# Blocks with one tile of tokens: the first expert product in another orientation, and two paddings

## The chip, the core and the metric

The kernel runs on one core of a Trainium2 chip. The metric is device time in microseconds (us) of that core, from runs of the whole program; one more execution was taken with the hardware profiler. The core has a matrix engine (TensorE; PE in the profile, PEld for its loads of the stationary operand), VectorE (DVE), ScalarE (ACT), GpSimd (POOL) and SyncE (SP, which issues most DMAs). A matmul holds a 128x128 stationary operand in the array and streams the moving operand past it; the result goes to PSUM.

## What is computed

Three stages follow each other on 4608 tokens of width 512:

```python
# chunked attention on q, k, v of (8, 8, 576, 64), chunks of 64; out -> x (4608, 512)
h = max(x @ w1, x @ w2, x @ w3); x = h @ w_out            # moe_: 512 -> 768 -> 512
e_idx = argmax(x @ w_gate, axis=1)                        # moe2_: 8 experts
gate_w = softmax(x @ w_gate)[row, e_idx]; eom = sigmoid(x @ w_output_gate)
for e in range(8):
    mask = e_idx == e
    h = maximum(x[mask] @ w1[e], 0)                       # 512 -> 1024
    out[mask] = gate_w[mask, None] * eom[mask, e, None] * (h @ w2[e])   # 1024 -> 512
```

## The kernel before

All products are in 32-bit floats, each as three matmuls: an operand is kept as a high part (rounded for the array) and a low part (the rest), and `mm3` (L101 to L104) multiplies high by high (L102), high by low (L103) and low by high (L104).

Up to some 710 us the kernel does attention and the first mixture, with instructions that a small planner in the program has put in order. In that stage tokens are taken in 9 blocks of 512; `moe_f` (L613) streams the tokens of block j, 512 columns, past 128x128 tiles of w1, w2, w3. There are 18 such tiles of 4 steps, so 18 x 4 x 3 = 216 matmuls for each of the 9 blocks. The tokens lie in `xt[j % 2]`, high and low part: `xth0`, `xtl0` for even j, `xth1`, `xtl1` for odd j. `moe_y` makes the product with w_out, 256 and 272 columns wide, 432 x 3 = 1296 matmuls, with tiles `ht` as the stationary operand.

Then come the experts. Tokens are sorted by expert and taken in blocks of at most 256 of one expert; block b holds one or two tiles of 128 tokens. `step(b)` does a block:

- `l1_mm`: for each of the 8 tiles of 128 hidden units, the weight tile is stationary and 256 token columns stream past it (4 steps x 3 matmuls): 96 matmuls into four PSUM banks (mm0, mm1, mm2, psg). `l1_hi` (ACT, relu) and `l1_lo` (DVE) put the result, hidden units on the partitions, into `hT` as high and low part. All 256 columns are computed whether the second tile has tokens or not.
- `x_T(b + 1)`: eight PE transposes turn the next block's tokens into `xs`, by way of the PSUM tile a2.
- `l2(b, t)`: for tile t, 24 matmuls of 512 columns with `hT` stationary and w2 moving; the result goes to tr0 (t = 0) or tr1. The second tile is inside `tc.If(full[b] > 0)`, a branch of PE alone: a block with one tile skips it.
- `y_act` (ACT) scales the result, `y_out` (POOL) scatters it to the output by an indirect DMA. `gather_ahead` (POOL) fetches the tokens of block b + 2.
- `switch(b, ns)`: where block b is the last of its expert (`lv > 0`), the weights of the next expert are converted from the raw tiles to high and low parts, `conv_hi` on ACT and `conv_lo` on DVE, four instructions each for every one of the four raw tiles; then SP issues `load_x` for the raw tiles of the expert after that, 1 MB each. Raw tiles 0 and 1 (w1) are converted inside the block, 2 and 3 (w2) at its end, behind `y_act(b, 1)`.

Each engine works through its own instructions in order and waits on semaphores. Tiles of the pool `p1` lie behind each other in SBUF in the order in which the program makes them; `xg01` (the gathered tokens) takes the place of `xth1` and is a little larger than it, 2 x 2 x 516 floats against 2048. The built program before puts the first weight tile `wpc0` at byte 20288 of a partition, `xth0` at 153472, `xtl0` at 161664, `xth1` at 169856 and `xtl1` at 178112.

Of the kernel before, what the change touches and what calls it, by code (L numbers as in the profile page):

```python
# [10 lines left out]
F32 = mybir.dt.float32  # L11
# [4 lines left out]
ACTF = mybir.ActivationFunctionType  # L16
# [5 lines left out]
def tile_chunk_attention_moe_moe(  # L22
# [16 lines left out]
    PE, ACT, DVE, POOL, SP = nc.tensor, nc.scalar, nc.vector, nc.gpsimd, nc.sync  # L39
# [55 lines left out]
    def f(ap):  # L95
        return ap.bitcast(F32)

    def sub(eng, o, a, b):
        eng.tensor_tensor(out=o, in0=a, in1=b, op=ALU.subtract)  # L99

    def mm3(o, ah, al, bh, bl, first, last):  # L101
        PE.matmul(o, ah, bh, start=first, stop=False)  # L102
        PE.matmul(o, ah, bl, start=False, stop=False)  # L103
        PE.matmul(o, al, bh, start=False, stop=last)  # L104
# [63 lines left out]
    def buf(shape, dtype, name):  # L168
        return p1.tile(shape, dtype, name=name, tag=name)
# [10 lines left out]
    pTF = [part(3, i, 1).rearrange("p (a c i) -> p a c i", a=HP, c=2) for i in range(2)]  # L180
    NV = len(v_buf)
    mxs, sms = ([buf([P, H], F32, f"{n}{i}") for i in range(NE2)] for n in ("mx", "sm"))
    XN = KD * TB * P
    xtn = lambda hl, i: f"xt{'hl'[hl]}{i}"
    xtile = lambda hl, i: p1.tile([P, KD, TB * P], F32R, name=xtn(hl, i), tag=xtn(hl, i))
# [593 lines left out]
    def xkeys(i, *hls):  # L779
# [6 lines left out]
        [("pTF", i) for i in range(2)] + [("cy", i) for i in range(2)],  # L786
    ]
    raw = [Late(ar, f"R{n}", [P, 4, DM], F32, f"raw{n}", akeys[n]) for n in range(4)]
    xg01 = Late(p1, xtn(0, 1 - lastx), [P, 2, 2, XW], F32, "xg01",
                xkeys(1 - lastx, 0) + [("xg", i, t) for i in range(2) for t in range(2)])  # L790
    xs0 = Late(p1, xtn(1, 1 - lastx), [P, 2, KD, BP], F32R, "xs0", xkeys(1 - lastx, 1) + [("xs0", i) for i in range(4)])
    xg2 = Late(wp, f"P{NFT // 4}", [P, 2, XW], F32, "xg2", [("w", n, hl) for n in range(16, NFT) for hl in range(2)])
# [23 lines left out]
    ]  # L816
    xsk = [[("xs0", i) for i in range(4)], [("wo", i) for i in range(8, 12)]]
    hTk = [("wo", i) for i in range(8)]
    xg = lambda b: xg2.t if b % NX == 2 else xg01.t[:, b % NX]
    yo = lambda b, t: yol[2 * (b % 2) + t].t  # L820
    bk = [("mm", 0), ("mm", 1), ("mm", 2), ("mm", 0)]
    ps_x = ps_a2.rearrange("p (a b) -> p a b", a=KD)
# [3 lines left out]
    def load_x(n, e, cond):  # L826
        src = (
            ew1_v[:, bass.ds(e, 1), :, n * DM:(n + 1) * DM] if n < 2
            else ew2_v[:, bass.ds(e, 1), (n - 2) * 4:(n - 1) * 4, :]
        )  # L830
        kw = {} if cond is None else {"cond": cond > 0}
        SP.dma_start(out=raw[n].t, in_=src.rearrange("p o k f -> p (o k) f"), **kw)

    def sval(engines, row, b, hi):
        return nc.values_load(  # L835
            sched_i()[0:1, row * NBLK + b:row * NBLK + b + 1], engines=engines, min_val=0, max_val=hi
        )
# [4 lines left out]
    def conv_lo(n, kk):  # L842
        sub(DVE, wx[n][:, 1, kk], raw[n].t[:, kk], f(wx[n][:, 0, kk]))
# [28 lines left out]
    def l1_mm(b, c, i):  # L872
        x, ps = xs[b % 2](), l1_ps(c)
        w, ff = wx[c // 2], ((2 * c + i) % 4) * P
        for kk in range(KD):
            mm3(
                ps[:, i], w[:, 0, kk, ff:ff + P], w[:, 1, kk, ff:ff + P], x[:, 0, kk], x[:, 1, kk],
                kk == 0, kk == KD - 1,
            )

    def l1_hi(c):
        ACT.activation(out=hT()[:, 0, 2 * c:2 * c + 2], in_=l1_ps(c), func=ACTF.Relu)  # L882

    def l1_lo(c):
        fs = slice(2 * c, 2 * c + 2)
        DVE.scalar_tensor_tensor(  # L886
            out=hT()[:, 1, fs], in0=l1_ps(c), scalar=0.0, in1=f(hT()[:, 0, fs]), op0=ALU.max, op1=ALU.subtract
        )

    def l2_mm(t, ff):  # L890
        sl = slice(t * P, (t + 1) * P)
# [6 lines left out]
    def y_act(b, t):  # L898
        ACT.activation(out=yo(b, t), in_=ps_y[t], func=ACTF.Copy, scale=xg(b)[:, t, DM:DM + 1])  # L899

    def y_out(b, t):
        POOL.indirect_dma_start(  # L902
            out=out, out_offset=bass.IndirectOffsetOnAxis(ap=ic[b % 4]()[:, t, 1:2].bitcast(U32), axis=0),
            in_=yo(b, t), in_offset=None, bounds_check=NT - 1, oob_is_err=False,
        )
# [223 lines left out]
    def x_T(b):  # L1129
        if b < NBLK:  # L1130
            xT_mm(b)
            for i in range(2):
                xT_hi(b, i)
                xT_lo(b, i)

    def switch(b, ns):


        lv, cl, en = meta[b]
        with tc.If(lv > 0):  # L1140
            for n in ns:
                for kk in range(4):
                    conv_hi(n, kk)
                    conv_lo(n, kk)
        for n in ns:
            load_x(n, en, cl)

    def scalars(b):
        meta[b] = (
# [9 lines left out]
    def l2(b, t):  # L1159
        for ff in range(2 * KD):  # L1160
            l2_mm(t, ff)
        if t == 0:
            y(b, t)

    def y(b, t):
        y_act(b, t)
        y_out(b, t)

    def step(b):
        scalars(b)  # L1170
        gather_ahead(b + 2)
        if b >= NB0:
            POOL.drain()  # L1173
        for c in range(4):
            for i in range(2):
                l1_mm(b, c, i)
            l1_hi(c)
            l1_lo(c)
            if c == 2:
                switch(b, (0,))  # L1180
        x_T(b + 1)
        switch(b, (1,))
        if b + 1 < NBLK:
            full[b + 1] = sval([ET.PE], 7, b + 1, 1)
        l2(b, 0)
        with tc.If(full[b] > 0):
            l2(b, 1)
        y(b, 1)
        switch(b, (2, 3))

    e1 = nc.values_load(next_i()[0:1, 0:1], engines=[ET.SP], min_val=0, max_val=E - 1)
    h0 = nc.values_load(next_i()[0:1, NBLK:NBLK + 1], engines=[ET.SP], min_val=0, max_val=1)
    for n in range(4):
        load_x(n, e1, h0)
    scalars(0)
    full = {1: sval([ET.PE], 7, 1, 1)}
    switch(0, (0,))
    l2(0, 0)
    x_T(1)
    switch(0, (1,))  # L1200
    l2(0, 1)
# [57 lines left out]
```

## Time and profile before

| | |
|---|---|
| median of 3 runs | 1191.08 us (1190.87 to 1193.05) |
| profiled execution | 1190.56 us |
| its span, first to last instruction | 1188.8 us |
| PE busy | 1172.4 us (99%) |
| PEld busy | 1035.3 us (87%) |
| DVE busy | 432.5 us (36%) |
| ACT busy | 416.3 us (35%) |
| POOL busy | 194.4 us (16%) |

The span is 1.8 us shorter than the profiled execution's own time: what lies around the instructions. A matmul's duration in the profile is longer than the distance to the next one, since matmuls are pipelined; so what a matmul costs is read from start to start. The granted TensorE clock was 0.998 over the span, where 1.0 is 2.4 GHz and 0.5 is 1.2 GHz.

### The profile page before, as it was taken

The numbers are of one execution on the slowest core, as the hardware profiler recorded it, in microseconds if no ns is written. First come the engines' busy times: TensorE is split into PE (matmuls) and PEld (weight loads), VectorE is DVE, ScalarE is ACT, GpSimd is POOL, SyncE is SP. The second block draws the span as 40 slices with busy tenths as digits, with TensorE's granted clock in tenths as the row PEclk, the third lists the DMA queues.
The fourth block names the chain that finished last, engine by engine and source line by source line (L and its number), as shares of the span: only waits on it lengthen the run. The fifth ranks groups of instructions, "written<-read, shape, count | busy, mean of one in ns | idle before, by whom it ended". The sixth has DMA issues, their size and how long they took to land. (4 is left out here: it accounts for less than half of the span.)

```text
span 1188.8 us, 23369 instructions
## 1 busy us (share of the span) xinstructions
PE 1172.4 (99%) x9219; PEld 1035.3 (87%) x9219; DVE 432.5 (36%) x1095; ACT 416.3 (35%) x1192; POOL 194.4 (16%) x243
## 2 busy tenths in 40 slices
PE   7999999999999999999999999999999999999997
PEld 6779889898898988989889898989999998998997
DVE  6995523232232322322223352121165221521172
ACT  5576323332333333333322321221266221521263
POOL 1000120211102111021110112212212211211212
PEclk9999999999999999999999999999999999999999
DMA  8753212112121121211230015211256411421151
GB/s 276 236 150 103 82 38 89 45 42 76 38 85 36 48 70 51 73 45 34 75 107 36 1 46 183 76 37 45 64 176 233 146 36 46 161 70 45 57 172 39
DMA packets 84317, 103.05 MB, mean 87 GB/s; under 512 B 40287, under 2 KB 49503, under 8 KB 84192
## 3 DMA queue, kind: packets, MB, share of 16 engines
q1 hardware_dynamic: 77152, 79.82, 21.0%
q0 software_dynamic: 7040, 21.60, 5.6%
q8 instruction: 75, 1.23, 0.4%
q14 instruction: 50, 0.41, 0.1%
HBM read 149.55 MB, written 20.52 MB: 143 GB/s over the span
## 5 line engine op out<-in xcount | busy, mean ns | idle before, releaser
L102 PE MATMUL mm<-xth,wpc 128*128 128x512 f32 x576 | 231.4, 402 | 0.0
L103 PE MATMUL mm<-xtl,wpc 128*128 128x512 f32 x576 | 226.3, 393 | 0.2 <-DVE xtl L99 0.2
L104 PE MATMUL mm<-xth,wpc 128*128 128x512 f32 x576 | 226.3, 393 | 0.0
L628 DVE TENSOR_TENSOR hs<-mm,hs 128x512 f32<-128x512 f32 x108 | 74.5, 690 | 226.9 <-PE mm L104 226.9
L886 DVE SCALAR_TENSOR_TENSOR wo<-mm,wo 128x512 fp32r<-128x512 f32 x64 | 43.6, 690 | 240.1 <-ACT wo L882 206.6
L104 PEld LDWEIGHTS mm<-xth,wpc 128*128 128x128 f32 x576 | 108.4, 188 | 24.5
L102 PEld LDWEIGHTS mm<-xth,wpc 128*128 128x128 f32 x576 | 108.2, 188 | 23.5
L103 PEld LDWEIGHTS mm<-xtl,wpc 128*128 128x128 f32 x576 | 108.4, 188 | 22.3 <-DVE xtl L99 0.5
L102 PE MATMUL mm<-wo,ht 128*128 128x256 f32 (+1 forms) x432 | 125.6, 291 | 0.0
L104 PE MATMUL mm<-wo,ht 128*128 128x256 f32 (+1 forms) x432 | 122.7, 284 | 0.0
L103 PE MATMUL mm<-wo,ht 128*128 128x256 f32 (+1 forms) x432 | 122.6, 284 | 0.0
L102 PE MATMUL tr<-wpc,wo 128*128 128x512 f32 x304 | 120.2, 396 | 0.0
L104 PE MATMUL tr<-wpc,wo 128*128 128x512 f32 x304 | 118.5, 390 | 0.0
L103 PE MATMUL tr<-wpc,wo 128*128 128x512 f32 x304 | 118.4, 389 | 0.0
L902 POOL DMA_INDIRECT out_dram<-yo,S x42 | 43.9, 1044 | 352.7 <-ACT yo L899 268.6
L99 POOL TENSOR_TENSOR ht<-hs,ht 128x512 fp32r<-128x512 f32 x48 | 61.9, 1290 | 192.3 <-ACT ht L630 192.3
L465 ACT ACTIVATE rg<-a,mx 128x64 f32<-128x64 f32 x264 | 79.3, 326 | 34.5 <-DVE mx L459 34.4
L99 DVE TENSOR_TENSOR wpc<-raw,wpc 128x512 fp32r<-128x512 f32 x112 | 70.3, 685 | 39.8 <-ACT wpc L840 39.8
L102 PEld LDWEIGHTS mm<-wo,ht 128*128 128x128 f32 x432 | 81.3, 188 | 1.3 <-issue 0.4
L882 ACT ACTIVATE wo<-mm 128x512 fp32r<-128x512 f32 x64 | 38.2, 598 | 124.8 <-PE mm L104 119.3
L103 PEld LDWEIGHTS mm<-wo,ht 128*128 128x128 f32 x432 | 81.5, 189 | 0.4
L104 PEld LDWEIGHTS mm<-wo,ht 128*128 128x128 f32 x432 | 81.3, 188 | 0.0
(243 smaller groups left out, 2252.7 us busy)
## 6 DMA issues: line engine op xcount, KB each, us to landing
raw<-in_moe_w_dram SPq DMA_DIRECT2D x92, 1024.0 KB
x_scratch<-U SPq DMA_DIRECT2D x36, 258.0 KB
rg<-in_q_dram SPq DMA_DIRECT2D x36, 256.0 KB
rg<-in_k_dram SPq DMA_DIRECT2D x36, 256.0 KB
wst<-in_moe_w_dram SPq DMA_DIRECT2D x18, 512.0 KB
rg<-in_v_dram SPq DMA_DIRECT2D x128, 64.0 KB
U<-in_moe_w_out_dram SPq DMA_DIRECT2D x6, 512.0 KB
rg<-in_v_dram SPq DMA_DIRECT2D x4, 256.0 KB
```

Source lines behind the costliest of these rows:

```text
L99: eng.tensor_tensor(out=o, in0=a, in1=b, op=ALU.subtract)
L102: PE.matmul(o, ah, bh, start=first, stop=False)
L103: PE.matmul(o, ah, bl, start=False, stop=False)
L104: PE.matmul(o, al, bh, start=False, stop=last)
L465: ACT.activation(out=ex[:, b, hp], in_=bank[b][:, hp], func=ACTF.Exp, scale=scale, bias=mx[:, HP * b + hp:HP * b + hp + 1], accum_out=sm[: ...
L628: add("DVE", t_dve(N), up, [pk, hk], [hk], lambda: DVE.tensor_tensor(out=h, in0=ps, in1=h, op=ALU.max))
L882: ACT.activation(out=hT()[:, 0, 2 * c:2 * c + 2], in_=l1_ps(c), func=ACTF.Relu)
L886: DVE.scalar_tensor_tensor(out=hT()[:, 1, fs], in0=l1_ps(c), scalar=0.0, in1=f(hT()[:, 0, fs]), op0=ALU.max, op1=ALU.subtract)
L902: POOL.indirect_dma_start(out=out, out_offset=bass.IndirectOffsetOnAxis(ap=ic[b % 4]()[:, t, 1:2].bitcast(U32), axis=0), in_=yo(b, t), in_ ...
```

## The change

In a block with one tile of tokens the first product is computed the other way round. The tokens are the stationary operand and w1 is the moving one, 512 columns wide (`h_mm`), so the result has tokens on the partitions; ACT takes the relu to SBUF (`h_relu`, in a part of the tile `U`), eight PE transposes bring it into two PSUM banks (`h_T`), and `hT_hi` (ACT) and `hT_lo` (DVE) write `hT` as before. Blocks with two tiles keep their instructions. For this the branch on `full[b]` now stands at the head of the block, on PE, ACT and DVE, with an Else; conversions are inside it, loads (`fetch`) behind it. Two paddings move tiles of `p1`: a tile of 48 floats behind the small attention tiles, and rows of 544 instead of 516 floats in `xg01`, which makes that slot 8704 bytes instead of 8256. The built program now has `xth0` at 153664, `xtl0` at 161856, `xth1` at 170048 and `xtl1` at 178752; `wpc0` stays at 20288.

```diff
--- before.py
+++ after.py
@@ -180,6 +180,8 @@
     pTF = [part(3, i, 1).rearrange("p (a c i) -> p a c i", a=HP, c=2) for i in range(2)]
     NV = len(v_buf)
     mxs, sms = ([buf([P, H], F32, f"{n}{i}") for i in range(NE2)] for n in ("mx", "sm"))
+
+    buf([P, 48], F32, "pad")
     XN = KD * TB * P
     xtn = lambda hl, i: f"xt{'hl'[hl]}{i}"
     xtile = lambda hl, i: p1.tile([P, KD, TB * P], F32R, name=xtn(hl, i), tag=xtn(hl, i))
@@ -786,7 +788,7 @@
         [("pTF", i) for i in range(2)] + [("cy", i) for i in range(2)],
     ]
     raw = [Late(ar, f"R{n}", [P, 4, DM], F32, f"raw{n}", akeys[n]) for n in range(4)]
-    xg01 = Late(p1, xtn(0, 1 - lastx), [P, 2, 2, XW], F32, "xg01",
+    xg01 = Late(p1, xtn(0, 1 - lastx), [P, 2, 2, 544], F32, "xg01",
                 xkeys(1 - lastx, 0) + [("xg", i, t) for i in range(2) for t in range(2)])
     xs0 = Late(p1, xtn(1, 1 - lastx), [P, 2, KD, BP], F32R, "xs0", xkeys(1 - lastx, 1) + [("xs0", i) for i in range(4)])
     xg2 = Late(wp, f"P{NFT // 4}", [P, 2, XW], F32, "xg2", [("w", n, hl) for n in range(16, NFT) for hl in range(2)])
@@ -816,7 +818,7 @@
     ]
     xsk = [[("xs0", i) for i in range(4)], [("wo", i) for i in range(8, 12)]]
     hTk = [("wo", i) for i in range(8)]
-    xg = lambda b: xg2.t if b % NX == 2 else xg01.t[:, b % NX]
+    xg = lambda b: xg2.t if b % NX == 2 else xg01.t[:, b % NX, :, 0:XW]
     yo = lambda b, t: yol[2 * (b % 2) + t].t
     bk = [("mm", 0), ("mm", 1), ("mm", 2), ("mm", 0)]
     ps_x = ps_a2.rearrange("p (a b) -> p a b", a=KD)
@@ -886,6 +888,32 @@
         DVE.scalar_tensor_tensor(
             out=hT()[:, 1, fs], in0=l1_ps(c), scalar=0.0, in1=f(hT()[:, 0, fs]), op0=ALU.max, op1=ALU.subtract
         )
+
+
+    hh = U[:, 0:2 * DM].bitcast(F32).rearrange("p (g n) -> p g n", g=2)
+
+    def h_mm(b, g):
+        x, w = xs[b % 2](), wx[g]
+        for kk in range(KD):
+            mm3(
+                ps_mm[g], x[:, 0, kk, 0:P], x[:, 1, kk, 0:P], w[:, 0, kk], w[:, 1, kk], kk == 0, kk == KD - 1
+            )
+
+    def h_relu(g):
+        ACT.activation(out=hh[:, g], in_=ps_mm[g], func=ACTF.Relu)
+
+    def h_T(g):
+        for i in range(4):
+            PE.transpose(ps_mm[2 + g][:, i * P:(i + 1) * P], hh[:, g, i * P:(i + 1) * P], ident)
+
+    def h_out(hl, g):
+        return hT()[:, hl, 4 * g:4 * g + 4, 0:P]
+
+    def hT_hi(g):
+        ACT.copy(h_out(0, g), ps_mm[2 + g].rearrange("p (a i) -> p a i", a=4))
+
+    def hT_lo(g):
+        sub(DVE, h_out(1, g), ps_mm[2 + g].rearrange("p (a i) -> p a i", a=4), f(h_out(0, g)))
 
     def l2_mm(t, ff):
         sl = slice(t * P, (t + 1) * P)
@@ -1133,17 +1161,22 @@
                 xT_hi(b, i)
                 xT_lo(b, i)
 
-    def switch(b, ns):
-
-
-        lv, cl, en = meta[b]
-        with tc.If(lv > 0):
+    def convs(b, *ns):
+
+        with tc.If(meta[b][0] > 0):
             for n in ns:
                 for kk in range(4):
                     conv_hi(n, kk)
                     conv_lo(n, kk)
+
+    def fetch(b, ns):
+
         for n in ns:
-            load_x(n, en, cl)
+            load_x(n, meta[b][2], meta[b][1])
+
+    def switch(b, ns):
+        convs(b, *ns)
+        fetch(b, ns)
 
     def scalars(b):
         meta[b] = (
@@ -1159,8 +1192,6 @@
     def l2(b, t):
         for ff in range(2 * KD):
             l2_mm(t, ff)
-        if t == 0:
-            y(b, t)
 
     def y(b, t):
         y_act(b, t)
@@ -1171,31 +1202,52 @@
         gather_ahead(b + 2)
         if b >= NB0:
             POOL.drain()
-        for c in range(4):
-            for i in range(2):
-                l1_mm(b, c, i)
-            l1_hi(c)
-            l1_lo(c)
-            if c == 2:
-                switch(b, (0,))
-        x_T(b + 1)
-        switch(b, (1,))
+        with tc.If(full[b] > 0) as both:
+            for c in range(4):
+                for i in range(2):
+                    l1_mm(b, c, i)
+                l1_hi(c)
+                l1_lo(c)
+                if c == 2:
+                    convs(b, 0)
+            x_T(b + 1)
+            convs(b, 1)
+            l2(b, 0)
+            y_act(b, 0)
+            l2(b, 1)
+        with both.Else():
+
+            for g in range(2):
+                h_mm(b, g)
+                if g:
+                    convs(b, 0)
+                h_relu(g)
+            for g in range(2):
+                h_T(g)
+                hT_hi(g)
+                hT_lo(g)
+            x_T(b + 1)
+            convs(b, 1)
+            l2(b, 0)
+            y_act(b, 0)
+        fetch(b, (0, 1))
         if b + 1 < NBLK:
-            full[b + 1] = sval([ET.PE], 7, b + 1, 1)
-        l2(b, 0)
-        with tc.If(full[b] > 0):
-            l2(b, 1)
+            full[b + 1] = sval(FULL, 7, b + 1, 1)
+        y_out(b, 0)
         y(b, 1)
-        switch(b, (2, 3))
+        convs(b, 2, 3)
+        fetch(b, (2, 3))
 
     e1 = nc.values_load(next_i()[0:1, 0:1], engines=[ET.SP], min_val=0, max_val=E - 1)
     h0 = nc.values_load(next_i()[0:1, NBLK:NBLK + 1], engines=[ET.SP], min_val=0, max_val=1)
     for n in range(4):
         load_x(n, e1, h0)
     scalars(0)
-    full = {1: sval([ET.PE], 7, 1, 1)}
+    FULL = [ET.PE, ET.Activation, ET.DVE]
+    full = {1: sval(FULL, 7, 1, 1)}
     switch(0, (0,))
     l2(0, 0)
+    y(0, 0)
     x_T(1)
     switch(0, (1,))
     l2(0, 1)
```

ACT, in the program before, one block in the expert stage from its first relu to the conversions at its end (L840 is `conv_hi`, L882 `l1_hi`, L862 the next block's tokens, L899 `y_act`; mm_156 to mm_158 and psg are the four banks):

```order
L882 ACTIVATE wo<-mm_156 128x512
L882 ACTIVATE wo<-mm_157 128x512
L882 ACTIVATE wo<-mm_158 128x512
L1140 COMPARE_AND_BRANCH
L840 CAST wpc_142<-raw_5878 128x512 x4
L1140 UNCONDITIONAL_BRANCH x2
L882 ACTIVATE wo<-psg 128x512
L862 CAST wo<-a_155 128x512 x2
L1140 COMPARE_AND_BRANCH
L840 CAST wpc_143<-raw_6006 128x512 x4
```

The four casts of raw tile 0 stand between the third relu and the fourth.

ACT, in the program after, the Else of a block (L903 is `h_relu`, L913 `hT_hi`, L842 `conv_hi`, L864 the next block's tokens, L927 `y_act`):

```order
L903 ACTIVATE U<-mm_157 128x512
L1166 COMPARE_AND_BRANCH
L842 CAST wpc_143<-raw_5879 128x512 x4
L1166 UNCONDITIONAL_BRANCH x2
L903 ACTIVATE U<-mm_158 128x512
L913 CAST wo<-mm_159 128x4x128
L913 CAST wo<-psg 128x4x128
L864 CAST wo<-a_156 128x512 x2
L1166 COMPARE_AND_BRANCH
L842 CAST wpc_144<-raw_6007 128x512 x4
L1166 UNCONDITIONAL_BRANCH x2
L927 ACTIVATE yo_7007<-tr_154,xg_6696 128x512
```

The same casts now stand between the first relu and the second of two, and what PE transposes next waits for that second relu.

PE, in the program after, the Else of a block from the end of the first product to the start of the second (L907 is `h_T`, L860 the next block's tokens, tr_154 the bank of the first tile's result):

```order
L102 MATMUL mm_158<-wpc_144,xs_6205 128x512
L103 MATMUL mm_158<-wpc_144,xs_6205 128x512
L104 MATMUL mm_158<-wpc_144,xs_6205 128x512
L907 MATMUL mm_159<-ident,U 128x128 x4
L907 MATMUL psg<-ident,U 128x128 x4
L860 MATMUL a_156<-ident,xg_6203 128x128 x8
L102 MATMUL tr_154<-wpc_145,wo 128x512
L103 MATMUL tr_154<-wpc_145,wo 128x512
L104 MATMUL tr_154<-wpc_145,wo 128x512
```

Eight transposes stand between the two products that were not there, and the eight of the next block's tokens come behind them.

## Rows read from the trace of the kernel before

**Rows 1.** Page, part 1: busy us, share of the span, instructions.

```profile
PE 1172.4 (99%) x9219; PEld 1035.3 (87%) x9219; DVE 432.5 (36%) x1095; ACT 416.3 (35%) x1192; POOL 194.4 (16%) x243
```

**Rows 2.** Source L1186, the skipped branch: duration ns, first and last start us.

```profile
L1186 PEldq EVENT_SEMAPHORE  x4: 51/51/51, 918.1 to 1159.3; - x4
```

**Rows 3.** Timeline of PE in the first one-tile block: start us, us, line, operation.

```profile
900.06 0.28 PE L102 MATMUL mm<-xs,wpc 128*128 128x256 f32 x1
...
911.58 1.04 PE L858 MATMUL a<-ident,xg 128*128 128x128 f32 x8
912.37 0.47 PE L102 MATMUL tr<-wpc,wo 128*128 128x512 f32 x1
...
918.23 0.36 PE L102 MATMUL mm<-wo,wpc 128*128 128x256 f32 x1
```

**Rows 4.** Timeline of PE, second product of a two-tile block, its second tile.

```profile
871.31 0.39 PE L102 MATMUL tr<-wpc,wo 128*128 128x512 f32 x1
...
876.75 0.28 PE L102 MATMUL mm<-wo,wpc 128*128 128x256 f32 x1
```

**Rows 5.** Timeline of PE, heads of the other one-tile blocks and their followers.

```profile
1011.50 0.28 PE L102 MATMUL mm<-wo,wpc 128*128 128x256 f32 x1
...
1029.68 0.36 PE L102 MATMUL mm<-xs,wpc 128*128 128x256 f32 x1
...
1122.83 0.28 PE L102 MATMUL mm<-xs,wpc 128*128 128x256 f32 x1
...
1141.17 0.38 PE L102 MATMUL mm<-wo,wpc 128*128 128x256 f32 x1 [0.31 <-PEq L1186]
...
1159.62 0.38 PE L102 MATMUL mm<-xs,wpc 128*128 128x256 f32 x1 [0.31 <-PEq L1186]
```

**Rows 6.** Windows, first and second one-tile block: length, busy us (instructions) by engine.

```profile
900.00:918.20 18.20, 18.08 (x129) 16.74 (x128) 13.58 (x22) 12.53 (x24) 4.12 (x4) 1.00 0.63 218
...
1011.50:1029.70 18.20, 18.05 (x130) 16.76 (x128) 8.86 (x14) 8.53 (x16) 3.18 (x4) 1.00 0.32 103
```

**Rows 7.** Timeline of ACT in the first, third and fourth one-tile block.

```profile
900.85 4.25 ACT L840 CAST wpc<-raw 128x512 fp32r<-128x512 f32 x8
905.00 0.59 ACT L882 ACTIVATE wo<-mm 128x512 fp32r<-128x512 f32 x1
...
909.45 2.17 ACT L840 CAST wpc<-raw 128x512 fp32r<-128x512 f32 x4
...
1125.97 0.60 ACT L882 ACTIVATE wo<-mm 128x512 fp32r<-128x512 f32 x1 [2.25 <-PE mm L104]
...
1142.06 4.26 ACT L840 CAST wpc<-raw 128x512 fp32r<-128x512 f32 x8
```

**Rows 8.** Timeline of PE, `moe_f`: an even block's 48 matmuls, an odd one's.

```profile
236.53 0.39 PE L102 MATMUL mm<-xth,wpc 128*128 128x512 f32 x1
...
247.52 0.39 PE L102 MATMUL mm<-xth,wpcr 128*128 128x512 f32 x1
...
311.55 0.40 PE L102 MATMUL mm<-xth,wpc 128*128 128x512 f32 x1
...
322.69 0.40 PE L102 MATMUL mm<-xth,wpcr 128*128 128x512 f32 x1
```

**Rows 9.** Sources L1186, L1214, L835: PE's sequencer, ns min/median/max, first and last start.

```profile
L1186 PEldq COMPARE_BRANCH  x1: 169/169/169, 872.7 to 872.7; - x1
...
L1214 PEldq COMPARE_BRANCH  x1: 3473/3473/3473, 1179.1 to 1179.1; - x1
...
L835 PEldq TENSOR_LOAD <-S x1: 299/299/299, 863.8 to 863.8; - x1
```

**Rows 10.** Windows near the start; the last three columns are PEclk, DMA share, GB/s.

```profile
16.50:19.90 3.40, 1.50 (x71) 1.27 (x72) 1.83 (x6) 2.37 (x6) 0.00 (x0) 0.99 1.07 369
19.90:23.30 3.40, 3.40 (x58) 3.09 (x59) 2.75 (x7) 1.68 (x9) 0.00 (x0) 0.51 1.09 377
```

**Rows 11.** Windows, from the issue of one raw weight load on.

```profile
1135.60:1140.60 5.00, 5.00 (x24) 4.00 (x22) 4.23 (x7) 3.08 (x6) 0.00 (x0) 1.00 0.60 210
```

## The prediction, made before the changed kernel ran

> **What bounds the kernel now.** I read the page first, then PE's timeline in the expert stage, then ACT's beside it. PE is busy 99% of the span and no other engine over 36% [rows 1]: a cut counts only if it takes time from PE and lets no other engine become late. Within a block PE runs without holes, so its cost is read from start to start. The skipped branch leaves one trace: its path ran four times, between 918 and 1159 us [rows 2], so four of the blocks have one tile. They reach from head to head: 18.17 us (900.06 to 918.23), 18.18 (1011.50 to 1029.68), 18.34 (1122.83 to 1141.17) and 18.45 (1141.17 to 1159.62) [rows 3, 5]. Each holds 96 first-product matmuls in 11.52 us, 120.0 ns each; the eight transposes of the next tokens, 0.79 us; and 5.86 us to the next head, of which at least 0.31 is PE idle where the skipped branch lets the engine run empty [rows 3, 5]. So 5.55 us are the second product with its start.
>
> **The first product.** 96 matmuls of 256 columns go, 24 of 512 come. The same form, token data stationary and a weight tile streaming 512 wide, is the second product of a two-tile block: 24 in 5.44 us, 226.7 ns each [rows 4]. So 11.52 becomes 5.44: minus 6.08 us per block.
>
> The Trainium skill, page "TensorE: Matmul & The Clock Gate", section "Wait — 56ns, not 53.3ns?", gives a full-speed matmul N / 2.4 GHz plus about 2.5 ns. By it the step would be an estimated 109.2 ns for 256 columns and 215.8 for 512, the cut 5.30 us per block, and the total 3.1 us smaller. The rows show 10.8 and 10.9 ns on top of that rule, so the rows are used.
>
> **The new transposes.** Four for each half: by the 0.79 us of eight [rows 3], 0.40 us per half; I take 0.44, since the second product's first matmul starts late behind them. They need the relu, and here ACT decides. An ACT relu begins 0.26 us after PE has passed on to the next group (1125.71, worked out as 1122.83 plus 24 steps, to 1125.97) and takes 0.60 [rows 5, 7]; the four casts that now stand between the two relus take 2.17 [rows 7].
>
> Where ACT is free at the head (second and third one-tile block; in the second ACT is busy 8.53 us against 12.53 in the first, the difference being the eight casts [rows 6, 7]), counted from the head: first relu 2.98 to 3.58, casts to 5.7, second relu 5.70 to 6.30, PE goes on at 6.40 (0.1 for the hand-over, an estimate from the 0.26 above less the matmul's drain). PE was done with the first half's transposes at 5.88, so 0.5 us idle. Then 0.44, 0.79 and 5.55: the next head at 13.2. Saved: 5.0 and 5.2 us.
>
> Where ACT comes in late (first and fourth: the block before was the last of its expert, so its eight casts of w2 run until 905.10 and 1146.32 [rows 7]): in the first, relu at 4.94 (905.00) to 5.54, casts to 7.6, second relu to 8.2, PE goes on at 8.3 after 2.4 us idle, next head at 15.1. Saved: 3.1 us. In the fourth the head also comes 0.47 us earlier against the casts, because the empty-engine gap ahead of it goes; relu 5.6, casts to 8.3, relu to 8.9, next head 15.8. Saved: 2.7 us. Together the four blocks give 16.0 us.
>
> What else lies there: the two stages from PSUM to `hT` stand on ACT and DVE beside x_T and the second product, which needs the first half after 0.79 us and the second 2.7 us later. The raw loads are issued after the casts, as before. From issue, 5 us at 210 GB/s are 1.05 MB, one load [rows 11]; the shortest distance from a load's issue to its cast, in the fourth block, is by my times some 10 us. The late casts of w2 are needed only by the next second product. I cost these at nothing; without that cover a late load holds the casts, the second relu behind them and so PE, us for us. In the order of SP and POOL nothing moves: the loads of raw tiles 0 and 1 wait for the same casts in a two-tile block, in a one-tile block for the copies into `hT` behind them, some 2 us more; the scatters wait for the same `y_act`.
>
> **The branch at the head.** PE's sequencer takes the jump at the end of a two-tile block at 872.7 us, 4.0 us ahead of the next head at 876.75 [rows 4, 9]. In that lead it now has a longer jump, the load of `full` (0.30 us) and the compare. The only far jump before, behind the last block, took 3.47 us [rows 9]. The sum stays under the lead: nothing, with 0 to 0.5 us per block as its bounds over 20 blocks, 0 to 10 us, and I take 0 because the ordinary jump row (0.169) is the nearer one.
>
> **The paddings.** These move every tile behind them, and the trace says that place matters. In the first mixture an even block's 48 matmuls take 10.99 us, 229.0 ns each, an odd one's 11.14 us, 232.1 each [rows 8]: same instructions, same weights, only the token tiles differ. By the addresses, modulo 256 bytes, weights lie at 64, even tokens at 128 and 128, odd ones at 128 and 192. In the second product both operands lie at 64, and the step is 226.7. After the change all token tiles lie at 64. If equal residues are the cause, 5 even blocks x 216 x 2.3 ns is 2.5 us and 4 odd x 216 x 5.4 is 4.7: 7.2 us. For the 1296 matmuls of `moe_y`, whose stationary tiles move too, no row shows the new place; bounded by the 2.3 ns between two residues, plus or minus 3.0 us; I take 0. Were equal residues no cause, the whole term lies between 0 and, if all blocks became like the odd ones, 1080 x 3.1 ns or 3.3 us lost.
>
> **The sum.** 16.0 and 7.2 are 23.2 us, off the profiled execution's 1190.56: 1167.4. That execution lies 0.5 under the median of the runs, so 1168.
>
> **Rivals.**
> (a) The paddings do nothing: 1175. For it: nothing in the trace shows the same tile at two places, and even against odd may have another cause. Against it: the difference returns in each of the nine blocks. The Trainium skill speaks for it: the page on the clock gate, section "Step-by-step: what each phase is for", gives PE two independent read ports, so that loading the next stationary tile takes nothing from the running matmul, and one operand's place against the other's would then not matter. Rows 8 show a difference that this rule has no room for. A worse place (token tiles and weights are still 256 bytes apart modulo 512) would give 1178 to 1181.
> (b) The clock falls in the one-tile blocks, where PE now has transposes and idle time for 2.2 to 4.1 us. Near the start PE was busy 1.50 of 3.40 us with transposes and small matmuls, and the next 3.4 us were granted 0.51, which is 1.2 GHz [rows 10]. At half speed such a stretch loses 1.7 us; in the two late blocks 3.4 us: 1171, in all four 1175. The same page, section "HAM oscillation — how this bites in real kernels", has the clock gated down again by such waits between bursts and each fall paid for anew. Against it: dense matmuls stand on both sides, and in two of the blocks the idle time is 0.5 us.
> (c) It becomes slower: the jump over the Else at the end of each of the 16 two-tile blocks among steps 1 to 20 is not covered. If the sequencer had no lead, 3.47 plus 0.30 would stand there 16 times, 60 us: 1228. From 1.45 us uncovered per block (23.2 / 16) the gain is gone. For it: the 3.47 us; against it: the 4.0 us of lead.
> (d) It does not do what it says, because conversions on ACT bind all four blocks as in the late ones: 4.7 us less, 1172.
>
> **How the numbers follow.** The forecast holds 0.50 (1163 to 1172); (a) 0.24, with 0.06 of it at the worse place; (b) 0.12; (d) 0.08; (c) 0.03; the other 0.03 is for something not seen, on either side. The range reaches from 1161, where ACT is never late (4.4 us) and `moe_y` gains its 3.0, to 1179, which takes in (a), (b) and (d) and part of the worse place. A measurement of this kernel can tell about 0.2%, 2.4 us, from no change. All cases but (c) and half of the unseen are faster by more: 0.94; within it 0.02; slower 0.04.
>
> **What would show it.** Right: in the four blocks 24 matmuls 226 to 227 ns apart, a hole of some 0.5 us ahead of the second four transposes in two of them and 2.4 to 3 us in the others, head to head 13 to 16 us; in `moe_f` one step of about 227 ns in even and odd blocks; no hole at other heads. Wrong: odd and even blocks still apart or slower, PE waiting at heads of two-tile blocks, a granted clock of 0.5 inside a one-tile block, or ACT's relu waiting for a raw load.

## The result, and the profile after

The changed kernel takes 1172.21 us (median of 4 runs, 1171.18 to 1175.55) against 1190.97 for the kernel before: ratio 0.9844, 95% interval 0.983 to 0.9859, faster by 18.8 us. Run again beside other kernels it took 1172.90 (0.986, 0.9845 to 0.9875). 1168 was predicted, with 1161 to 1179 as its range, so the time lies 4 us over the forecast and inside the range. The profiled execution took 1175.55 us with a span of 1173.8; it is the slowest of its four, and the reason for that is one of the findings.

PE is still what bounds it. Page, part 1, the line that answers to [rows 1]:

```profile
PE 1151.7 (98%) x8963; PEld 1014.3 (86%) x8963; DVE 428.1 (36%) x1087; ACT 414.7 (35%) x1192; POOL 195.4 (17%) x243
```

Timeline of PE in the four one-tile blocks, which answers to [rows 3, 5]: start us, us, line, operation, and in brackets the idle time before it and what ended that:

```profile
898.86 0.39 PE L102 MATMUL mm<-wpc,xs 128*128 128x512 f32 x1
...
904.46 0.66 PE L907 MATMUL mm<-ident,U 128*128 128x128 f32 x4
907.01 1.05 PE L907 MATMUL psg<-ident,U 128*128 128x128 f32 x4 [1.90 <-ACT U L903]
907.86 1.91 PE L860 MATMUL a<-ident,xg 128*128 128x128 f32 x8
909.42 0.78 PE L102 MATMUL tr<-wpc,wo 128*128 128x512 f32 x1
...
915.50 0.28 PE L102 MATMUL mm<-wo,wpc 128*128 128x256 f32 x1
...
1008.97 0.47 PE L102 MATMUL mm<-wpc,wo 128*128 128x512 f32 x1
...
1015.43 0.66 PE L907 MATMUL psg<-ident,U 128*128 128x128 f32 x4 [0.30 <-ACT U L903]
...
1022.26 0.28 PE L102 MATMUL mm<-xs,wpc 128*128 128x256 f32 x1
...
1115.45 0.39 PE L102 MATMUL mm<-wpc,xs 128*128 128x512 f32 x1
...
1128.65 0.39 PE L102 MATMUL mm<-wpc,wo 128*128 128x512 f32 x1
...
1134.82 0.66 PE L907 MATMUL mm<-ident,U 128*128 128x128 f32 x4 [0.56 <-ACT U L903]
1137.38 0.66 PE L907 MATMUL psg<-ident,U 128*128 128x128 f32 x4 [1.90 <-ACT U L903]
...
1144.21 0.28 PE L102 MATMUL mm<-xs,wpc 128*128 128x256 f32 x1
```

Head to head: 16.64, 13.29, 13.20 and 15.56 us, 58.69 where there were 73.14. In each, TensorE waits for ACT's second relu (L903): 0.30 us where ACT is free, 1.90 where it comes in late. In the fourth it waits 0.56 us for the first relu as well. The eight transposes of the next tokens (L860) take 1.56 us to the next row in the first block; [rows 3] have 0.79. Windows of the changed kernel show why (length, busy us by engine in the order of [rows 6], then PEclk, DMA share, GB/s), here for the first block and for two places near the start:

```profile
904.95:907.13 2.18, 0.28 (x3) 0.12 (x2) 2.17 (x5) 2.18 (x5) 0.98 (x1) 1.00 1.04 373
907.13:910.54 3.41, 3.41 (x15) 3.22 (x16) 2.00 (x4) 1.47 (x3) 0.00 (x0) 0.50 1.03 382
...
29.90:33.31 3.41, 3.41 (x56) 3.10 (x54) 3.11 (x7) 2.20 (x4) 0.00 (x0) 0.50 0.67 189
87.93:91.34 3.41, 3.41 (x11) 2.79 (x10) 3.41 (x9) 2.83 (x5) 0.00 (x0) 0.50 0.87 209
```

Behind the hole the granted clock is 0.5, 1.2 GHz, for 3.41 us, and near the start there are two such stretches more than the one that the trace of before has [rows 10].

Timeline of ACT in the first block, beside [rows 7]:

```profile
899.65 4.26 ACT L842 CAST wpc<-raw 128x512 fp32r<-128x512 f32 x8
903.81 0.60 ACT L903 ACTIVATE U<-mm 128x512 f32<-128x512 f32 x1
904.30 2.17 ACT L842 CAST wpc<-raw 128x512 fp32r<-128x512 f32 x4
906.36 0.60 ACT L903 ACTIVATE U<-mm 128x512 f32<-128x512 f32 x1
```

Eight casts of the block before, the first relu at 4.95 us from the head, four casts, the second relu at 7.50; TensorE goes on at 8.15.

In `moe_f` the even block and the odd one are alike now; timeline of PE over the same 48 matmuls as [rows 8]:

```profile
239.19 0.39 PE L102 MATMUL mm<-xth,wpc 128*128 128x512 f32 x1
...
250.07 0.39 PE L102 MATMUL mm<-xth,wpcr 128*128 128x512 f32 x1
...
313.49 0.39 PE L102 MATMUL mm<-xth,wpc 128*128 128x512 f32 x1
...
324.37 0.39 PE L102 MATMUL mm<-xth,wpcr 128*128 128x512 f32 x1
```

10.88 us for 48 in both, 226.7 ns each; before 229.0 and 232.1.

To see where the time went, the span of each profiled execution is cut at starts on PE: (A) the first 1200 matmuls, to the start of the next, (B) on to the head of the second expert block, (C) to the head of the first one-tile block, (D) the four one-tile blocks, (E) the blocks between them, (F) from the last head to the end. Times in us; the other columns are experiments told below.

| stage | before | before again | changed | changed again | order alone | paddings alone | all at 128 |
|---|---|---|---|---|---|---|---|
| A | 104.8 | 104.5 | 108.5 | 105.3 | 106.1 | 106.3 | 104.3 |
| B | 632.2 | 632.2 | 627.3 | 627.0 | 632.4 | 627.2 | 627.4 |
| C | 163.1 | 163.1 | 163.1 | 163.1 | 163.1 | 163.1 | 163.1 |
| D | 73.1 | 73.1 | 58.7 | 58.5 | 57.2 | 73.1 | 57.1 |
| E | 186.4 | 186.5 | 186.7 | 186.6 | 186.5 | 186.6 | 186.6 |
| F | 29.1 | 29.4 | 29.6 | 29.8 | 29.6 | 29.2 | 29.8 |

The changed kernel against before: A plus 3.7, B minus 4.9, D minus 14.4, E and F plus 0.8 together. With the rounding that is the 14.9 us by which the span is shorter, and the two profiled executions are 15.0 apart (1190.56 and 1175.55). So the two parts of the change are at work at their own places, and A gives back 3.7.

### The profile page after: what moved, and what is told of

Its sections match the earlier page's. It is cut to its first block, busy times and chain, and to the rows that moved or that the text cites. A ratio compares the mean times of both kernels' runs of the same rounds, so it can differ in the third digit from the quotient of the medians.

```text
span 1173.8 us, 22891 instructions
## 1 busy us (share of the span) xinstructions
PE 1151.7 (98%) x8963; PEld 1014.3 (86%) x8963; DVE 428.1 (36%) x1087; ACT 414.7 (35%) x1192; POOL 195.4 (17%) x243
## 4 chain that ended last, share of the span: by engine, by line
PE 90%; DVE 4%; DMA 2%; issue 2%; ACT 1%; POOL 0%; POOLq 0%; SPq 0%; DVEq 0%; ACTq 0%
PE mm L102 21%; PE mm L103 20%; PE mm L104 20%; PE tr L102 6%; PE tr L104 6%; PE tr L103 6%; DMA wst<-in_moe_w_dram 2%; PE a L519 2%; PE a L860 2%; PE a L439 1%; PE psg L104 1%; PE psg L103 1%; PE psg L102 1%; PE tr L494 1%; ACT wpc L842 1%
## 5 line engine op out<-in xcount | busy, mean ns | idle before, releaser
L888 DVE SCALAR_TENSOR_TENSOR wo<-mm,wo 128x512 fp32r<-128x512 f32 x52 | 35.5, 690 | 202.3 <-ACT wo L884 159.6
L927 ACT ACTIVATE yo<-tr,xg 128x512 f32<-128x512 f32 x42 | 28.5, 689 | 143.2 <-PE tr L104 143.2
```

The lines of the kernel that those rows point to most:

```text
L888: DVE.scalar_tensor_tensor(out=hT()[:, 1, fs], in0=l1_ps(c), scalar=0.0, in1=f(hT()[:, 0, fs]), op0=ALU.max, op1=ALU.subtract)
```

## The experiments

**The order alone.** The new block without the paddings.

```diff
-    buf([P, 48], F32, "pad")
-    xg01 = Late(..., [P, 2, 2, 544], F32, "xg01", ...)
+    xg01 = Late(..., [P, 2, 2, XW], F32, "xg01", ...)
-    xg = lambda b: xg2.t if b % NX == 2 else xg01.t[:, b % NX, :, 0:XW]
+    xg = lambda b: xg2.t if b % NX == 2 else xg01.t[:, b % NX]
```

> The new one-tile block without the two paddings. By the trace of the changed kernel the four one-tile blocks give 14.5 us and the dense steps before 709 us give nothing once the stretch up to 97 us is counted. Theory (the two further clock falls and the stall before 97 us come with the moved tiles): one clock fall before 100 us, moe_f at 229.0 and 232.1 ns as before, time 1191.0 - 14.5 = 1176.5 us. Rival (they come with the longer program, that is with the new block): three falls before 100 us, and 1176.5 + 4.7 = 1181 us. Rival of the recorded prediction (a), paddings do nothing: no different from the changed kernel, 1172 us.

Measured: 1176.80 us, ratio 0.9884 (0.9869 to 0.9899): 14.1 us less than its own runs of before. `moe_f` stays at 229.0 and 232.2 ns, with one clock fall before 100 us. The first one-tile block, timeline of PE:

```profile
901.61 0.40 PE L102 MATMUL mm<-wpc,xs 128*128 128x512 f32 x1
...
909.75 0.66 PE L906 MATMUL psg<-ident,U 128*128 128x128 f32 x4 [1.90 <-ACT U L902]
...
916.59 0.28 PE L102 MATMUL mm<-wo,wpc 128*128 128x256 f32 x1
```

The same hole of 1.90 us, no fall behind it, 14.98 us from head to head. The four blocks give 73.14 - 57.18 = 16.0 us; the difference to 14.1 lies in A and F. The time fits my first theory, but the runs below take its reason away.

**The paddings alone.**

```diff
+    buf([P, 48], F32, "pad")
+    xg01 = Late(..., [P, 2, 2, 544], F32, "xg01", ...)
+    xg = lambda b: xg2.t if b % NX == 2 else xg01.t[:, b % NX, :, 0:XW]
```

> The kernel before with the two paddings and nothing else. Theory (equal residues give 226.7 ns in moe_f, and the moved tiles also bring the early clock falls): moe_f at 226.7 in even and odd blocks, three clock falls before 100 us, 1191.0 - 7.2 + 4.7 = 1188.5 us. Rival (the early falls come with the new block): moe_f at 226.7, one fall, 1191.0 - 7.2 = 1183.8 us. Rival (a), paddings do nothing: 1191 us.

Measured: 1187.15 us, 0.9966 (0.9952 to 0.998): 4 us less. Stage B is 5.0 us shorter, as in every kernel with these paddings, and `moe_f` shows 226.7 ns. Rival (a) is out. The falls are two (at 17.80 for 6.83 us and at 86.06 for 3.41), neither the one nor the three that the theories named.

**The casts behind.** The four casts of raw tile 0 go behind the copies into `hT`.

```diff
             for g in range(2):
                 h_mm(b, g)
-                if g:
-                    convs(b, 0)
                 h_relu(g)
...
             x_T(b + 1)
-            convs(b, 1)
+            convs(b, 0, 1)
```

> The changed kernel with the four casts of raw tile 0 moved from between the two relus to behind the copies into hT. Theory (these casts, between the two relus on ACT, make the hole ahead of the second four transposes): relu 1 ends 0.6 us after relu 0, PE's hole of 1.9 us in the first and fourth one-tile block goes, the clock fall in the first goes with it, each of the four blocks takes 12.8 to 13.1 us from head to head; 58.7 falls to some 52 us, 6.7 less: 1172.2 - 6.7 = 1165.5 us. Rival (the backlog of ACT before relu 0 decides, not these casts): the late blocks stay at 15 us or more, 1171 to 1172 us. Rival (the moved casts come too late for the next block's first product): a hole of some 2 us at the heads behind the four blocks, 8 us given back, 1172 to 1174 us.

Measured: 1167.35 us, 0.9811 (0.9797 to 0.9824), 1.8 us over the theory's sum. First and fourth block, timeline of PE:

```profile
894.48 0.39 PE L102 MATMUL mm<-wpc,xs 128*128 128x512 f32 x1
...
900.06 0.66 PE L907 MATMUL mm<-ident,U 128*128 128x128 f32 x4
900.81 0.66 PE L907 MATMUL psg<-ident,U 128*128 128x128 f32 x4
...
907.65 0.28 PE L102 MATMUL mm<-wo,wpc 128*128 128x256 f32 x1
...
1120.63 0.39 PE L102 MATMUL mm<-wpc,wo 128*128 128x512 f32 x1
...
1127.30 0.66 PE L907 MATMUL mm<-ident,U 128*128 128x128 f32 x4 [1.07 <-ACT U L903]
...
1134.63 0.28 PE L102 MATMUL mm<-xs,wpc 128*128 128x256 f32 x1
```

The hole of 1.90 is gone and the first block takes 13.17 us. In the fourth block, 14.00 us, the wait for the first relu grows from 0.56 to 1.07 us, the backlog of ACT that a rival named. The third block takes 13.20 us as before, but its eight casts now stand together ahead of its `y_act`, which begins 0.71 us behind the fourth head (1121.34 against 1120.63) where the changed kernel has 0.20 (1128.85 against 1128.65). So 0.5 us of what the move gained comes back there. The second and third block stay at 13.29 and 13.20 with their hole of 0.30, since there the second relu waits for its own product. Stage D is 53.7, where the theory had 52, and 3.4 less than in a run with both holes and no fall in these blocks (57.1, "all at 128"). No hole opens at the next heads: E is 186.5.

**All at 128.** Weights and tokens both moved by 64 bytes.

```diff
+    const.tile([P, 16], F32, name="pad0")
     gwr = const.tile([P, KD, 2 * E], F32, name="gwr")
```

> The changed kernel with 64 bytes more ahead of every tile: weights and tokens both at 128 modulo 256 instead of 64. Theory (what counts is that moving and stationary tiles have the same residue): moe_f stays at 226.7 ns, time as the changed kernel, 1172 us. Rival (the place 64 itself is good, 128 is bad): moe_f at 229 ns or more, 1175 us or more.

Measured: 1170.91 us (2 runs, 0.9834, 0.9816 to 0.9852). `moe_f`: the odd block's 48 matmuls take 10.88 us, 226.7 ns, as at 64. This execution has the shortest A (104.3) and no fall in D, although both late blocks have their holes of 1.90. So it stands for the changed kernel without falls in the four blocks.

**The changed kernel and the kernel before, again.** Nothing edited.

> The changed kernel once more, nothing edited. Theory (the clock falls at 30, 88 and 907 us and the late weight loads before 56 us are chances of one execution): the head of the first one-tile block comes at 895 to 897 us instead of 898.86, that block takes 15.0 us (16.64 less the 1.7 of the fall), the time is 1170 to 1172 us. Rival (they belong to this kernel): the same falls at the same places, the head at 898 to 899 us, 1173 to 1176 us.

> The kernel before once more, nothing edited, for its first 105 us. Theory (what is lost there is a chance of one execution): the 1200th matmul starts anywhere between 104 and 108.5 us, as in the other traces. Rival (the kernel before has no such loss): at 104.8 us again, with one clock fall.

Measured: the changed kernel 1172.90 us, 0.9 over the theory's range; the first head comes at 895.45 and its block takes 15.00 us without a fall (the theory), but now the fourth has one. Window of its trace, columns as above:

```profile
1131.81:1135.22 3.41, 2.96 (x13) 2.96 (x14) 2.33 (x4) 1.56 (x4) 2.15 (x2) 0.50 1.06 394
```

That block takes 17.00 us instead of 15.56. Stage A is 105.3, not 108.5. So the places and the number of the falls change from one execution of the same kernel to the next. The kernel before gave 1190.53 us and A 104.5, with one fall, at 28.90 instead of 19.85. Its A was close to the first both times; over all twelve traces A lies between 104.3 and 109.8 (the latter in the run with x_T between, told below).

A also differs by the arrival of loads: waits of ACT in 40:57 us, first the changed kernel (us in total, times, longest), then "all at 128", whose program differs in addresses alone:

```profile
ACT U L550 <- DMA wst<-in_moe_w_dram: 2.8, 1, 2.8
ACT rg L550 <- DMA wst<-in_moe_w_dram: 2.3, 2, 1.9
```

```profile
ACT U L551 <- DMA wst<-in_moe_w_dram: 0.4, 1, 0.4
```

The weight tiles of the first mixture arrive later in one execution than in the other, by 4.7 us of ACT's waiting. ACT's waits for DVE in the same stretch are shorter in turn (the two longest 2.6 us together against 4.4). How much of this reaches TensorE was not separated.

**Tokens at 0.** On the run with the casts behind: 32 numbers of padding instead of 48, tokens at 0 modulo 256, weights at 64.

```diff
-    buf([P, 48], F32, "pad")
+    buf([P, 32], F32, "pad")
```

> As the run with the casts behind, but the padding is 32 numbers instead of 48: token tiles at 0 modulo 256, weights still at 64. Theory (equal residues give the short step): moe_f at 229 ns or more in all blocks, 2.6 to 5.2 us more than with the casts behind, so 1170 to 1172.5 us. Rival (only the places 128 and 192 are bad): 226.7 to 227.8 ns, 1167.4 us.

Measured: 1176.82 us (2 runs, 0.9885, 0.9867 to 0.9903), 9.5 over the run with the casts behind, about twice what I expected. Timeline of PE, 48 matmuls of `moe_f` and 96 of a first product with `xs0`:

```profile
313.44 0.40 PE L102 MATMUL mm<-xth,wpc 128*128 128x512 f32 x1
...
324.64 0.40 PE L102 MATMUL mm<-xth,wpcr 128*128 128x512 f32 x1
...
941.06 0.28 PE L102 MATMUL mm<-xs,wpc 128*128 128x256 f32 x1
...
952.37 1.04 PE L860 MATMUL a<-ident,xg 128*128 128x128 f32 x8
```

11.20 us or 233.3 ns a step, in all blocks, longer than any before: a place that is not equal to the weights' is bad even where it is neither 128 nor 192. The theory had no row for tokens 64 below the weights and took the steps it knew. And a surprise: the 256-wide first product is faster there, 11.31 us for 96 or 117.8 ns, where equal residues have 119.9.

**x_T between.** On the run with the casts behind, the transposes of the next tokens go between the two halves.

```diff
-            for g in range(2):
-                h_T(g)
-                hT_hi(g)
-                hT_lo(g)
-            x_T(b + 1)
+            h_T(0)
+            xT_mm(b + 1)
+            h_T(1)
+            for g in range(2):
+                hT_hi(g)
+                hT_lo(g)
+            ...
```

> As the run with the casts behind, but the eight transposes of the next tokens stand between the two halves of the new transposes on TensorE. Theory (relu 1 ends 0.46 us after the first half's transposes in the second and third block and 0.26 in the first, and this hole is what is filled): the second product starts 0.25 to 0.45 us earlier in the three blocks, about 1 us in all: 1166.4 us. Rival (the second product waits for DVE's part of hT of the first half, which doesn't move): no change, 1167.4 us. Rival (the conversions of the next tokens on ACT and DVE come between and are late at the next head): 1168 us or more.

Measured: 1165.38 us, 0.9784 (0.9771 to 0.9798). Second one-tile block, timeline of PE:

```profile
1005.98 0.39 PE L102 MATMUL mm<-wpc,wo 128*128 128x512 f32 x1
...
1011.42 0.60 PE L907 MATMUL mm<-ident,U 128*128 128x128 f32 x4
1011.86 1.04 PE L860 MATMUL a<-ident,xg 128*128 128x128 f32 x8
1012.73 0.60 PE L907 MATMUL psg<-ident,U 128*128 128x128 f32 x4
1013.09 0.48 PE L102 MATMUL tr<-wpc,wo 128*128 128x512 f32 x1
...
1018.69 0.28 PE L102 MATMUL mm<-xs,wpc 128*128 128x256 f32 x1
```

No hole is left there, 12.71 us. The first and third take 12.86 and 12.76; the fourth grows to 14.49, since it comes 0.44 us sooner after the third and its wait for ACT's backlog is 1.63 now. D is 52.8, 0.8 less; the theory had 1 us. The medians differ by 2.0, more than these blocks give.

**The experts' tokens at 0.** On the run before this: both tiles of experts' tokens at 0 modulo 256, everything else in its place.

```diff
+    xg01 = Late(..., [P, 2, 2, 528], F32, "xg01", ...)
+    xs0 = Late(..., [P, 2 * KD * BP + 64], F32R, "xs0", ...)
+        lambda: xs0.t[:, 48:48 + 2 * KD * BP].rearrange(...),
+        lambda: wo_t[0]...[:, 4144:6192].rearrange(...),
```

> As the run with x_T between, but the two tiles of the experts' tokens lie at 0 modulo 256 instead of 64; the weights stay at 64. In the run with tokens at 0 the 256-wide first product with tokens in xs0 took 117.8 ns a step, and 119.9 with those in wo, which lay at 64. Theory (for 256 columns the moving tile at 0 against the stationary at 64 is the shorter step, the opposite of 512 columns): all first products of the two-tile blocks at 117.8; 17 blocks x 96 x 2.1 ns = 3.4 us less, the 24 steps of the one-tile blocks at 229.0 instead of 226.7, 0.2 us more: 1165.4 - 3.2 = 1162.2 us. Rival (it was the tile xs0 and not its place): wo's first products stay at 119.9, some 1.7 us less, 1163.7. Rival (the gain of place does not add up on the path): 1165.4.

Measured: 1163.12 us, 0.9765 (0.975 to 0.978), the fastest version. A first product whose tokens lie in `wo`, timeline of PE:

```profile
906.96 0.28 PE L102 MATMUL mm<-wo,wpc 128*128 128x256 f32 x1
...
918.27 1.04 PE L860 MATMUL a<-ident,xg 128*128 128x128 f32 x8
```

11.31 us for 96, 117.8 ns, in `wo` as in `xs0`. It is the place and not the tile. C and E, where the first products of two-tile blocks lie, are together 3.1 us shorter than in the run before this (theory: 3.4); the medians differ by 2.3. The 24 steps of a one-tile block, where the weights now lie 64 above the stationary tokens, average 229 ns as the theory had it: 5.52 us in the second block (999.36 to 1004.88) against 5.44. So a moving tile 64 above the stationary one has the same step here as the tokens of `moe_f` had before, with the roles of tokens and weights exchanged.

**The casts twice.** The changed kernel with the four casts done twice between the relus.

```diff
                 if g:
-                    convs(b, 0)
+                    convs(b, 0, 0)
```

> The changed kernel with the four casts of raw tile 0 done twice between the two relus (the same values again). Theory (the casts hold the second relu and PE us for us): the hole ahead of the second four transposes grows by 2.2 to 2.6 us, from 1.9 to 4.1 or more in the first and fourth one-tile block and from 0.46 to 2.7 or more in the second and third; 4 x 2.3 = 9 us more, 1181 to 1182 us. On the clock: if such a hole makes it fall, one-tile blocks with 0.5 show in this trace in more than one block and the time is up to 4 x 1.7 us higher, 1188; rival (the fall in these blocks is a chance not tied to the hole's length): none or one. Rival on the place (ACT has room behind the casts, so that they cost less than their time): 1175 us or less.

Measured: 1183.75 us (3 runs, 0.9943, 0.9923 to 0.9962). Timeline of PE, then windows of the same trace, columns as above:

```profile
900.58 0.66 PE L907 MATMUL mm<-ident,U 128*128 128x128 f32 x4
905.21 0.66 PE L907 MATMUL psg<-ident,U 128*128 128x128 f32 x4 [3.98 <-ACT U L903]
...
1015.20 0.76 PE L907 MATMUL psg<-ident,U 128*128 128x128 f32 x4 [2.21 <-ACT U L903]
```

```profile
906.39:909.80 3.41, 3.41 (x12) 2.73 (x11) 2.50 (x5) 2.21 (x5) 0.00 (x0) 0.50 0.89 282
1015.62:1019.03 3.41, 3.41 (x15) 3.12 (x13) 2.32 (x4) 1.17 (x3) 0.00 (x0) 0.50 0.20 35
1141.91:1148.74 6.83, 5.98 (x20) 5.28 (x21) 5.16 (x9) 4.22 (x9) 1.47 (x1) 0.50 0.56 192
```

The holes grow by 2.08 us in the two late blocks and 1.91 in the others, the time of the added casts. The clock falls around the end of three of the four holes (1.18 and 0.42 us behind it in the first and second block, 0.85 ahead of it in the fourth), in the fourth block for 6.83 us. So the rival "none or one" is out, though the third block's hole, as long as the second's, has no fall. D is 71.0, 13.9 more than in "all at 128": 8.0 for the casts, the rest the falls (1.6, 1.6 and 2.8 us).

Holes and falls in the one-tile blocks, all traces together: of eight holes ahead of the second four transposes of about 1.90 us (two each in the changed kernel twice, the order alone and all at 128) two have a fall around their end; of the four of 2.21 to 3.98 three; of those of 0.30 us and the four waits of 1.07 to 1.63 us for a first relu none. Twelve long holes are few: that a longer one is more often followed by a fall is a hint, that only the long ones are is clearer.

## Why the prediction came out as it did

**First product, transposes, ACT: right.** For the four blocks 15.1, 13.2, 13.2 and 15.8 us were worked out, 57.3 together; the two traces without a fall in D have 57.2 and 57.1. The chain itself was right: relus at 4.95 and 7.50 us after the first head (4.94 and 7.6 expected), TensorE on at 8.15 (8.3). The 16.0 us are what the order gives. The holes were sized less well: 0.30 and 1.90 us idle where 0.5 and 2.4 to 3 were to show. The 2.4 us took the end of the first four transposes from the blocks where ACT is free (5.88); behind a relu that ends at 5.54 they end at some 6.1, which leaves 2.2. The heads, which the 16.0 us rest on, do not depend on this figure.

**Branch at the head: right.** C and E, with all the heads of two-tile blocks in them, change by at most 0.3 us. Rival (c) did not occur, nor did (d): the free blocks stayed at 13.2 and 13.3. F, which no term of the sum covered, is 0.5 longer in the changed kernel. To the start of TensorE's last matmul it takes 23.0 us before and 23.1 after (1159.62 to 1182.66, 1144.21 to 1167.30), so the difference lies behind that; its cause stays open.

**Paddings: cause right, size too large.** The step "all at 64 gives 226.7 ns" holds to the digit in the 48 matmuls shown, and B is 5.0 us shorter where 7.2 were expected for the whole. The mis-sized term is the product 216 x 2.3 and 216 x 5.4: [rows 8] are 48 of the 216 steps of a block, the undisturbed ones. Summed over a block, an even one fell from 50.39 to 50.08 us and an odd one from 50.97 to 50.08, that is 0.31 and 0.89 where 0.50 and 1.17 stood in the sum. At the start of a block and around the places where attention instructions stand between its matmuls, some 40 steps take 229 to 236 ns with equal residues as without. For the nine blocks, 5 x 0.31 + 4 x 0.89, this is 5.1. The term for `moe_y`, taken at 0 with 3.0 either way, came out at 0: its 1296 steps sum to 161.8 us in both traces, with the stationary tiles `ht` at 192 modulo 256 before and at 64 after.

The Trainium skill, page "TensorE: Matmul & The Clock Gate", section "Step-by-step: what each phase is for", gives TensorE two independent read ports and has the loading of the next stationary tile take no bandwidth from the running matmul. The same instructions at 226.7, 229.0 and 233.3 ns with nothing but an address moved do not agree with that as a statement on time.

**Rival (b) occurred beside the forecast.** I gave it 0.12 as a case of its own; by the runs it is a chance that each late block has, two of eight. In the profiled execution it cost 1.6 us (16.64 against 15.0), in the second profile 1.4. The Trainium skill, page "TensorE: Matmul & The Clock Gate", section "HAM oscillation — how this bites in real kernels", has the waits for loads between bursts of matmuls gate the clock down at every one of them. The runs agree in part: falls follow holes, three of four in the run with the casts twice, but not every hole, and six of the eight of 1.90 us had none.

**What I did not have.** The first 105 us differ from execution to execution by up to 5.5 us. The traces show both clock falls there and weight tiles that arrive at other times; by what shares was not separated, and the falls do not settle it alone: the run with the order alone has one fall and an A of 106.1, the one with the casts behind has 6.83 us at half clock and 104.3. I took the one profile of before for the stretch's fixed length.

The sum with the sizes as measured: 16.0 + 5.0 - 0.7 (E and F) = 20.3 us, 1190.6 - 20.3 = 1170.3. The profiled execution of "all at 128" has 1169.95. The rest to 1172.2 and 1172.9 I put down to falls and the start, which only the profiled execution of each shows. The granted clock recorded with each run points the same way: 0.992 to 0.996 in the changed kernel's eight, 0.997 and 0.996 in the two of "all at 128". By an estimate from the windows above, one stretch of 3.41 us at half clock takes 3.41 x 0.5 / 1173, or 0.0015, off it. Whether the eight had more of them by more than chance stays open: the other kernel ran twice only.

## What to carry to other kernels

Where an in-order engine stands between two products of TensorE, only what the next product needs belongs ahead of it; the same casts a few instructions later left 3.4 us more, and gave back 0.5 through ACT's backlog at the next head. A gain per step that is read from the undisturbed steps of a loop is too large for the whole loop, here 7.2 for 5.0: sum over the whole loop first. And a hole of about two us on TensorE is priced with what may follow it, here 1.4 to 1.6 us lost at half clock in some of the executions.

## What the runs showed of the hardware

The step of a matmul stream whose stationary tile is loaded anew for each matmul depends on the two operands' byte addresses against each other. Moving less stationary, modulo 256, at 512 columns: 0 gives 226.7 ns (both at 64 or both at 128), 64 gives 229.0 (in `moe_f` before, and in the one-tile blocks of the run with the experts' tokens at 0), minus 64 gives 233.3, and 64 and 128 by turns 232.1. These are means over the three matmuls of `mm3`: at 64, in `moe_f` before, they take 232, 226 and 229. At 256 columns it is not the equal place that is best: 0 gives 119.9, minus 64 gives 117.8, and 128, where `xs0` lay in the kernel before, 120.0 [rows 3]. So of the distances tried the best is not the same for both widths; others were not tried. Whether the two are also equal modulo 512 makes no difference that shows: the tokens of `moe_f` lie 256 from the weights (153664 and 20288), the two operands of the second product are equal (`hT` begins at 94016), and both have 226.7. Why the distance matters stays open.

A version with the casts behind, x_T between and the experts' tokens at 0 takes 1163.12 us, 27.5 under the kernel before and about 9 under the changed one. What is left in its four blocks is one wait for ACT's backlog in the fourth.
